# Turning the combine weights in 32x32 blocks on VectorE, and sending the output by thirds of the tokens

## The chip, the cores and the metric

One core of one Trainium2 chip runs the whole program. The metric is the device time of one execution in microseconds (us), taken as the median of several runs. TensorE (PE, with its weight loads shown apart as PEld), VectorE (DVE), ScalarE (ACT), GpSimd (POOL) and the queue engine SyncE (SP) each run their own instruction stream in order; DMA moves data between main memory and the on-chip memories (SBUF, and PSUM, into which TensorE accumulates).

## What is computed

Attention over 4 batches x 8 heads x 768 tokens with head size 64, in which a query sees only the keys whose 6 sign bits equal its own; its output, as 3072 tokens x 512, goes through a soft mixture of 8 experts with 4 slots each. The part that the change touches is the end:

```python
logits = x @ phi                       # 3072 x 32 slots
slot_input = softmax(logits, axis=0).T @ x
for e in range(8):
    slot_out[e] = np.maximum(slot_input[e] @ w1[e], 0) @ w2[e]
c = softmax(logits, axis=1)            # "combine weights", 3072 x 32
out = c @ slot_out                     # 3072 x 512
```

w1 and w2 are 33.5 MB together and come in 64 pieces of 512 KB; the output is 6.3 MB and leaves in 12 pieces of 512 KB.

## The kernel before

**Attention, heads 0 to 31.** Each head takes six "slots" of a hand-made plan: the tables STEADY and ONCE give every step (`smax`, `scores`, `av`, `one_add`, `load_weights` and so on) a time in slots, and the steps are written out in the order of these times, so each engine gets its instructions in that order. `smax` (L418 on TensorE, L421 and L424 on VectorE) finds row maxima, `scores` (L465, exponentials on ScalarE at L469) the weights, `av` (L494) the weighted values. After the last slot of a batch the logits of its 768 tokens are at hand: `batch_weigh` and `batch_share` (L750 to L761) turn them into combine weights and keep them in the SBUF tile `call`, tokens on the partitions.

**End of attention.** Heads 30 and 31 are finished one by one: `one_sum`, `one_turn`, `one_rec`, `one_log`, `one_x` on TensorE, `one_fold` (L623, L624), `one_add` (L630, L634) and `one_put` (L643) on VectorE. Then come the softmax over all tokens (`batch_max` L665, `batch_top`, `batch_fold` L736 to L743) and the slot inputs `siT`.

**Experts.** `hidden` (L904, first layer, groups g = 0 and 1 of four experts), `above_zero` and `turned` (transposes on TensorE, L918), then `model` (L986, second layer) for the left half of the columns (x = 0) and the right half (x = 1). `split_out` (L992 on ScalarE, L993 on VectorE) leaves the slots' outputs as a rounded part and what the rounding left, and `send` (L1008) multiplies them with the turned combine weights `cts`: TensorE into PSUM, VectorE and ScalarE copy out (L1010), SP issues one output piece of 512 KB (L1011) for 128 columns q and 1024 tokens n.

**Turning the combine weights.** `send` needs the slots on the partitions, in a high and a low part. ScalarE and VectorE split `call` into two parts (L934, L935); `arrange` copies them for three blocks of 128 tokens into one tile `avs`, eight small copies shared by VectorE and GpSimd (L943); `turn_weights` turns these blocks by three matmuls with the identity (L949, tile `qa`) and ScalarE copies the result out of PSUM (L950). There are eight such groups (24 blocks); `more_weights(1)` puts one at a time between pieces of `hidden` and `model`, and all eight stand ahead of the first `send`.

**Weights.** `load_weights` asks SP for the next piece (L192 for w1, L194 for w2) as buffers come free: pool wa holds 23, then wb 5, wy 6, wp 3, wl 5 and wc 1 as the tiles of attention are given up, three pieces go into the tile `xq` after its last use, ten into wa after the first `hidden`, eight more after the second. The outputs come behind all of these in SP's stream; six buffers of wy serve them, one of them holding `split_out`'s halves.

Of the kernel before, what the change touches and what calls it, by code (L numbers as in the profile page):

```python
# [9 lines left out]
F32 = mybir.dt.float32  # L10
F32R = mybir.dt.float32r
# [23 lines left out]
N_WA, N_WB, N_WY, N_WP, N_WL, N_WC = 23, 5, 6, 3, 5, 1  # L35
# [43 lines left out]
    ('acc', 31, 1): 189.7, ('acc', 31, 2): 189.705, ('av', 31, 2, 0): 191.864, ('av', 31, 2, 1): 192.733,  # L79
    ('batch_exp', 3): 195.721, ('batch_max', 3): 195.72, ('batch_scale', 3): 195.724, ('batch_top',): 195.7215,  # L80
    ('batch_top_exp',): 195.7222, ('batch_turn', 3): 195.723, ('bits', 2): -3.273955249,
    ('bits_rest',): -37.319143276, ('copy_ident',): -68.066444498, ('first_bits',): -103.791174563,
    ('first_last',): -38.392596163, ('first_mz',): -40.0, ('first_rows', 1): -74.359163702,
    ('first_rows', 2): -26.360163702, ('first_x', 0): -24.334455598, ('first_x', 1): -27.067989537,
    ('first_y', 2): -36.763070462, ('keep_warm', 'a'): -76.154870356, ('keep_warm', 'c'): 195.7225,
    ('load', 10): 37.688669, ('load', 12): 49.688669, ('load', 14): 61.688669, ('load', 2): -12.762070462,
    ('load', 4): 3.305061249, ('load', 6): 13.688669, ('load', 8): 25.688669, ('load_phi',): 10.931086823,
    ('load_v', 0): -61.78673, ('load_weights', 0): 26.669343, ('load_weights', 1): 27.9087,
# [12 lines left out]
    ('scores', 18, 0, 1): 109.396684, ('scores', 20, 0, 1): 121.396684, ('scores', 3, 2, 0): 19.21665,
    ('scores', 5, 2, 0): 31.21665, ('scores', 6, 0, 1): 37.396684, ('scores', 7, 2, 0): 43.21665,
    ('scores', 8, 0, 1): 49.396684, ('scores', 9, 2, 0): 55.21665, ('shift_rows', 0): -3.614750908,
    ('smax', 0, 0, 0): -48.201477503, ('smax', 1, 0, 0): -0.414889731, ('smax', 1, 0, 1): -0.455916355,
    ('smax', 1, 1, 0): -0.415889731, ('smax', 1, 1, 1): -2.391596163, ('smax', 1, 2, 0): 1.521154004,
    ('smax', 1, 2, 1): 0.801484107, ('smax', 1, 3, 0): 0.906213766, ('smax', 1, 3, 1): 0.217376722,
    ('smax', 1, 4, 0): -0.202477503, ('smax', 1, 4, 1): 0.380833062, ('smax', 1, 5, 0): 0.541771494,
    ('smax', 1, 5, 1): -1.142037598, ('split_hi', 2): -7.827923536, ('split_lo', 0, 0): -56.921030823,
    ('split_lo', 0, 1): -46.209390463, ('split_lo', 2, 0): -3.471460996, ('split_lo', 2, 1): -1.544050507,
    ('spread_bits', 1): -11.457228506, ('spread_bits', 2): 2.576813849, ('spread_l', 0): -24.414889731,  # L110
    ('spread_l', 1): -11.211767025, ('spread_l', 2): 9.582727007, ('spread_x', 0): -2.418272993,
    ('spread_x', 1): 3.415989498, ('spread_x', 2): 9.118993846, ('spread_y', 1): -58.753320164,
# [960 lines left out]
```

## Time and profile before

| | us |
|---|---|
| median of 3 runs | 481.88 (481.84 to 482.64) |
| the profiled execution | 480.13 |
| its span (first to last instruction) | 478.4 |
| PE busy | 461.8 (97%) |
| DVE busy | 364.4 (76%) |
| POOL busy | 330.5 (69%) |
| ACT busy | 250.3 (52%) |

The profiled execution is 1.75 us under the median of the runs; about 1.7 us of it lie outside the span. The granted TensorE clock is 1.00 of full speed in every stage from 60 to 470 us. A timeline row gives start, duration, engine, line and operation, the number of merged instructions and in brackets the idle time before it with what ended it. A merged row spans from the first start to the last end.

### The profile page before, as it was taken

To read this page: it belongs to the slowest core of one execution; us is meant where nothing else is said; L and a number is where in the kernel's file an instruction comes from. 1 tells how busy PE (TensorE), PEld (TensorE's weight loads), DVE (VectorE), ACT (ScalarE), POOL (GpSimd) and SP (SyncE) were. 2 spreads that over 40 slices of the span, in tenths; PEclk is the share of its full clock that TensorE was granted. 3 is DMA by queue.
4 is the path that set the end of the run, shared out by engine and by line. 5 is a ranking of instruction groups with operands and counts; after the bars stand their busy time and mean duration, and the time that the engine had idled before them with its cause. 6 is when DMAs were issued, how large, how long until landed. Compare 5 with 4: busy or idle time off the path is not lost.

```text
span 478.4 us, 10738 instructions
## 1 busy us (share of the span) xinstructions
PE 461.8 (97%) x4012; PEld 290.6 (61%) x4012; DVE 364.4 (76%) x690; ACT 250.3 (52%) x465; POOL 330.5 (69%) x236
## 2 busy tenths in 40 slices
PE   7799999999999999999999999999999999989992
PEld 4466666666666666666666565656656666453581
DVE  5658897979798888888888888888989766463242
ACT  4365555564666464555655564646655455431242
POOL 7868776969595969696868696968859696602200
PEclk9799999999999999999999999999999999999998
DMA  5668587868575757777767676767758388979967
GB/s 149 186 164 198 145 180 218 181 170 185 172 174 160 161 136 160 224 173 209 189 168 196 173 216 167 213 166 224 195 169 223 112 214 317 393 295 388 408 267 299
DMA packets 39697, 99.71 MB, mean 208 GB/s; under 512 B 7422, under 2 KB 13708, under 8 KB 39644
## 3 DMA queue, kind: packets, MB, share of 16 engines
q1 hardware_dynamic: 39260, 98.16, 71.6%
q0 software_dynamic: 224, 0.47, 0.5%
q8 instruction: 32, 0.52, 0.5%
q10 hardware_dynamic: 160, 0.39, 0.3%
q14 instruction: 21, 0.17, 0.1%
HBM read 52.76 MB, written 6.29 MB: 123 GB/s over the span
## 4 chain that ended last, share of the span: by engine, by line
PE 90%; DMA 2%; POOL 2%; DVE 2%; issue 1%; ACT 1%; SPq 1%; DVEq 0%; ACTq 0%; POOLq 0%
PE st L465 29%; PE av L494 27%; PE smx L418 15%; PE qh L904 3%; PE mi L556 3%; PE mi L506 2%; PE mi L521 2%; PE qs L986 2%; PE mi L357 2%; DMA out<-w 1%; PE mi L541 1%; PE mi L711 1%; PE qa L949 1%; POOL stage L321 1%; PE mi L449 1%
## 5 line engine op out<-in xcount | busy, mean ns | idle before, releaser
L482 POOL TENSOR_TENSOR acc<-acc,pt 128x768 f32<-128x768 f32 x125 | 229.2, 1834 | 9.1
L469 ACT ACTIVATE pt<-st 128x512 f32<-128x512 f32 x288 | 164.1, 596 | 49.0 <-PE st L465 41.0
L465 PE MATMUL st<-XY 128*128 128x512 f32 (+1 forms) x768 | 180.1, 346 | 0.0
L424 DVE TENSOR_REDUCE mx<-smx 128x1 f32<-128x512 f32 x192 | 130.6, 688 | 28.8 <-PE smx L418 25.3
L465 PEld LDWEIGHTS st<-XY 128*128 128x128 f32 x768 | 129.5, 190 | 16.3 <-issue 0.6
L494 PE MATMUL av<-pt,v 128*32 128x384 f32 x1536 | 136.2, 488 | 0.0
L418 PE MATMUL smx<-XY 96*128 96x256 f32 (+1 forms) x384 | 117.8, 360 | 1.6 <-DMA XY<-bt 0.7
L476 POOL TENSOR_TENSOR acc<-pt 128x768 f32<-128x768 f32 x32 | 58.7, 1835 | 65.8 <-ACT pt L469 65.8
L494 PEld LDWEIGHTS av<-pt,v 128*32 128x32 f32 x1536 | 46.4, 110 | 70.7 <-issue 70.5
L418 PEld LDWEIGHTS smx<-XY 96*128 96x128 f32 x384 | 68.7, 191 | 29.6 <-DVE mx L424 8.8
L421 DVE TENSOR_REDUCE mx<-smx 128x2 f32<-128x512 f32 x96 | 64.8, 675 | 4.3 <-PE smx L418 3.8
L498 ACT COPY avs<-av 128x384 f32<-128x384 f32 x32 | 15.3, 478 | 89.9 <-PE av L494 89.9
L318 DVE TENSOR_REDUCE stage<-stage 128x768 fp32r<-128x1536 f32 x28 | 50.1, 1790 | 0.0
L513 DVE RECIPROCAL sm<-sm 128x128 f32<-128x128 f32 x45 | 38.1, 896 | 0.0
L558 DVE TENSOR_TENSOR xq<-mi,r 128x256 f32<-128x256 f32 x45 | 17.6, 418 | 26.2 <-PE mi L556 26.2
L311 ACT ACTIVATE stage<-stage 128x768 fp32r<-128x768 f32 x30 | 24.9, 840 | 9.0 <-DMA stage<-qk 6.7
L556 PEld LDWEIGHTS mi<-ident,avs 128*128 128x128 f32 x90 | 10.2, 141 | 10.6 <-issue 10.0
L509 ACT ACTIVATE sm<-mi,eps 128x384 f32<-128x384 f32 x15 | 8.7, 582 | 13.8 <-PE mi L506 13.8
L943 POOL CAST avs<-lacc 128x48 fp32r<-128x48 f32 x8 | 2.1, 266 | 19.6 <-ACT lacc L934 12.5
L556 PE MATMUL mi<-ident,avs 128*128 128x128 f32 x90 | 15.7, 282 | 0.0
L986 PE MATMUL qs<-w 128*32 128x128 f32 (+1 forms) x360 | 15.5, 305 | 0.0
L904 PE MATMUL qh<-w,siT 128*32 128x512 f32 x128 | 14.6, 595 | 0.0
(179 smaller groups left out, 334.6 us busy)
## 6 DMA issues: line engine op xcount, KB each, us to landing
w<-w SPq DMA_DIRECT2D x61, 512.0 KB
XY<-stage SPq DMA_DIRECT2D x62, 384.0 KB
stage<-qk SPq DMA_DIRECT2D x32, 384.0 KB
XY<-stage SPq DMA_DIRECT2D x62, 192.0 KB
v<-vt SPq DMA_DIRECT2D x32, 192.0 KB
out<-w SPq DMA_DIRECT2D x12, 512.0 KB
xq<-w SPq DMA_DIRECT2D x3, 512.0 KB
XY<-bt SPq DMA_DIRECT2D x62, 19.5 KB
```

Of the source, the lines that this page charges most:

```text
L318: nc.vector.tensor_reduce(out=w[:, 2 * x + 1], in_=stage[:, x:n + 1:n - x].rearrange("p t s -> p s t"), axis=AX.X, op=ALU.add, negate=True)
L418: nc.tensor.matmul(pt[:, o:o + b - a], Ys[h % N_Y][0:96, 0, t * P:(t + 1) * P], Ys[h % N_Y][0:96, 1, a:b], start=True, stop=True)
L421: nc.vector.tensor_reduce(out=mx[:, n - 1:n + 1], in_=pt.rearrange("p (a x) -> p a x", a=2), axis=AX.X, op=ALU.max)
L424: nc.vector.reduce_max(out=mx[:, n:n + 1], in_=pt, axis=AX.X)
L465: nc.tensor.matmul(pt[:, o:o + b - a], x[:, 1, i * P:(i + 1) * P], x[:, 0, a:b], start=first, stop=not first)
L469: nc.scalar.activation(pts[i // 2][:, 512 * u:512 * u + 512], pt, AF.Exp, scale=D ** -0.5)
L476: nc.gpsimd.tensor_tensor(out=s["acc"], in0=pr[:, 0:S], in1=pr[:, S:2 * S], op=ALU.add)
L482: eng.tensor_tensor(out=s["acc"], in0=s["acc"], in1=pr[:, a * S:(a + 1) * S], op=ALU.add)
L494: nc.tensor.matmul(s["av"][D * c + d:D * c + d + 32, 0:HC], s["v"][:, i, d:d + 32], pr[:, o + c * HC:o + (c + 1) * HC], start=(i == 0), st ...
L513: nc.vector.reciprocal(out=rs[:, k * P:(k + 1) * P], in_=rs[:, k * P:(k + 1) * P])
L556: nc.tensor.transpose(pt[:, o:o + P], st[h + a]["avs"][:, k * P:(k + 1) * P], ident)
L904: nc.tensor.matmul(ph[fh][32 * j:32 * j + 32], siT[:, k, 4 * g + j, :], wt[0, g, k, j][:, fh * 512:(fh + 1) * 512], start=(k == 0), stop=( ...
```

## The change

The combine weights no longer pass through TensorE. `batch_share` now leaves them in `call` already split (one more copy on ScalarE, one more subtraction on GpSimd or, for the last batch, VectorE, both 128x192), laid out so that the 16 numbers of a token for two expert groups lie side by side. `combine(n, j, q)` turns for a third of the plan (n = 0 and 1: nine blocks of 128 tokens each, n = 2: six) one 32-partition strip with a VectorE transpose of 32x32 blocks (L794), `combine_round(n)` copies the turned tile to the matmul's format on ScalarE (L802). Rounds 0 and 1 stand in the plan of attention, at slots 178 to 194; round 2, with the last batch, stands in the expert stage after the transposes of the hidden layer. `phi`'s columns, the folding constant and `siT` are permuted to match.

`send` takes a list of thirds: the first two column quarters go out third by third with pieces of `model` between them, and a part of the third quarter goes out ahead of the last `model`. The output buffers are in wb. Of the weights, wb now takes 7, wy 3, wc 2, and one piece goes into the transposes' tile `cr`; the tile XY2 has a pool of its own (yq), freed early; wa serves 16 instead of 18 later tiles.

```diff
-N_WA, N_WB, N_WY, N_WP, N_WL, N_WC = 23, 5, 6, 3, 5, 1
+N_WA, N_WB, N_WY, N_WP, N_WL, N_WC = 23, 7, 3, 3, 5, 2
...
+    ('combine', 0, 0, 0): 181.507650263, ('combine', 0, 0, 1): 184.14604213, ('combine', 0, 0, 2): 186.99190093,
...
+    ('combine_round', 1): 193.790766733, ('copy_ident',): -68.066444, ('first_bits',): -103.791175,
...
-    call = cp.tile([P, B, 3, 2, NS], F32, name="call")
+    call = cp.tile([P, B - 1, 3, 2, 4, 2, 2 * SPE], F32, name="call")
...
     def batch_share(b):
-        cb = call[:, b]
+        cb, hb = share_of(b), share_of(b, 0).bitcast(F32R)
...
+        nc.scalar.copy(hb, cb)
+        eng.tensor_tensor(out=cb.bitcast(F32R), in0=cb, in1=hb, op=ALU.subtract)
+
+    def combine(n, j, q):
+        t0, t1 = n * N_H, min((n + 1) * N_H, B * NT)
+        if n not in turned_shares:
+            turned_shares[n] = (ep.tile([P, N_H * P], F32, name="cr", bufs=1) if n < 2 else piece())[:, 0:(t1 - t0) * P]
+        o = t0 % (2 * N_H)
+        src = tiles[32 * q:32 * q + 32, o:o + t1 - t0, j]
+        nc.vector.transpose(out=turned_shares[n][32 * j:32 * j + 32].rearrange("r (t q k) -> r t q k", q=4, k=32)[:, :, q],
+                            in_=src[:, :, None].broadcast_to([32, t1 - t0, 2, 4 * SPE]))
+
+    def combine_round(n):
+        if n % 2 == 0:
+            cts[n // 2] = (piece() if n else ep.tile([P, 2 * N_H * P], F32, name="ct")).bitcast(F32R)
+        t = turned_shares[n]
+        o = n % 2 * N_H * P
+        nc.scalar.copy(cts[n // 2][:, o:o + t.shape[1]], t)
...
             free_pp()
+            free_yq()
+            ep = ctx.enter_context(tc.tile_pool(name="ep", bufs=1))
             wb = ctx.enter_context(tc.tile_pool(name="wb", bufs=N_WB))
...
+            load_piece(turned_shares[1][:, 0:F])
             load_weights(wc, N_WC)
...
-    def arrange(t0):
-    def turn_weights(t0, ca):
-    def more_weights(n):
...
     turned(hs1, hT1)
+    for j in range(4):
+        for q in range(4):
+            combine(2, j, q)
+    combine_round(2)
     model(po0, 0, 0, range(4, FC))
-    more_weights(1)
-    model(po0, 0, 1, range(4))
-    more_weights(1)
-    model(po0, 0, 1, range(4, FC))
+    model(po0, 0, 1)
     so0 = split_out(po0, 0)
-    more_weights(1)
     model(po1, 1, 0, range(4), left)
-    more_weights(1)
-    model(po1, 1, 0, range(4, FC), left)
-    more_weights(1)
-    send(so0[:, left], 0)
-    send(so0[:, right], 1)
-    model(po1, 1, 1, cols=left)
+    for n in range(3):
+        send(so0[:, left], 0, (n,))
+        send(so0[:, right], 1, (n,))
+        if n < 2:
+            model(po1, 1, n, range(4 - 4 * n, FC), left)
     so1 = split_out(po1, 1, left)
     po2 = po_tile(P)
     model(po2, 1, 0, cols=right)
-    send(so1, 2)
+    send(so1, 2, (0, 1))
     model(po2, 1, 1, cols=right)
-    send(split_out(po2, 1, right), 3)
+    so2 = split_out(po2, 1, right)
+    send(so1, 2, (2,))
+    send(so2, 3)
```

How the instructions stand on two engines, before and now. VectorE at the end of attention, before, from the last sums of head 31's weights (`acc1`) to the first step that needs head 31's logits (`dl` from `st`); `lacc` holds the batch's logits, `r1` reciprocals of sums:

```order
L482 TENSOR_TENSOR acc1_86<-acc1_86,pt1_83 128x768
L482 TENSOR_TENSOR acc1_86<-acc1_86,pt2_84 128x768
L588 TENSOR_SCALAR r1_4988<-mi_4984 128x6
L592 RECIPROCAL r1_4988<-r1_4988 128x6
L623 COPY sm_5000<-lacc_4324 64x384
L624 TENSOR_TENSOR lacc_4324<-lacc_4324,sm_5000 64x384
L630 TENSOR_TENSOR dl_4951<-dl_4951,mi_5021 64x384
L634 TENSOR_TENSOR lacc_4324<-lacc_4324,dl_4951 64x384
L643 TENSOR_TENSOR xq_4326<-mi_5037,r1_4988 128x3x2x64
L590 COPY r1_5064<-smx_5060 128x6
L591 SCALAR_TENSOR_TENSOR r1_5064<-r1_5064,smx_5060 128x6
L592 RECIPROCAL r1_5064<-r1_5064 128x6
```

VectorE at the same place now; the tile `cr_4988` is the second round's, in the buffer of the first:

```order
L794 STREAM_TRANSPOSE cr_4988<-call_116 32x9x32 x9
L602 TENSOR_SCALAR r1_5029<-mi_5025 128x6
L606 RECIPROCAL r1_5029<-r1_5029 128x6
L496 TENSOR_TENSOR acc1_89<-acc1_89,pt1_86 128x768
L794 STREAM_TRANSPOSE cr_4988<-call_116 32x9x32
L496 TENSOR_TENSOR acc1_89<-acc1_89,pt2_87 128x768
L794 STREAM_TRANSPOSE cr_4988<-call_116 32x9x32
L657 TENSOR_TENSOR xq_4335<-mi_5016,r1_5029 128x3x2x64
L794 STREAM_TRANSPOSE cr_4988<-call_116 32x9x32 x5
L604 COPY r1_5129<-smx_5125 128x6
L605 SCALAR_TENSOR_TENSOR r1_5129<-r1_5129,smx_5125 128x6
L606 RECIPROCAL r1_5129<-r1_5129 128x6
```

Sixteen transposes stand among these steps, and the four steps on `lacc` and `dl` that stood ahead of head 31's reciprocals now follow them, ahead of the step on head 31's logits:

```order
L637 COPY sm_5133<-lacc_4333 64x384
L638 TENSOR_TENSOR lacc_4333<-lacc_4333,sm_5133 64x384
L644 TENSOR_TENSOR dl_4995<-dl_4995,mi_5118 64x384
L648 TENSOR_TENSOR lacc_4333<-lacc_4333,dl_4995 64x384
L644 TENSOR_TENSOR dl_4995<-st_5147,avs_5145 64x384
```

Before, a reciprocal step and a wait for TensorE stood between the fourth of these rows and the fifth; now nothing does.

TensorE before, from the end of the first `model` to the first `send` (`qs` is `model`'s tile, `qa<-ident,avs` one group of turned weights, L1008 the output):

```order
L986 MATMUL qs<-w 32x256 x2
L949 MATMUL qa<-ident,avs 128x128 x3
L986 MATMUL qs<-w 32x128 x16
L949 MATMUL qa<-ident,avs 128x128 x3
L986 MATMUL qs<-w 32x128 x16
L949 MATMUL qa<-ident,avs 128x128 x3
L1008 MATMUL qh<-w 128x512
L1008 MATMUL qh<-w 128x256 x2
L1008 MATMUL qa<-w 128x512
```

TensorE now, from the same place (`ct` and `w` on the right hold the turned weights):

```order
L996 MATMUL qs<-w 32x256
L996 MATMUL qs<-w 32x128 x16
L1018 MATMUL qh<-ct,w 128x512 x4
L996 MATMUL qs<-w 32x128 x16
L1018 MATMUL qa<-ct,w 128x512
L1018 MATMUL qh<-ct,w 128x512
L1018 MATMUL qa<-ct,w 128x512
L1018 MATMUL qh<-ct,w 128x512
L996 MATMUL qs<-w 32x128 x32
```

The groups of three are gone, and the first four output matmuls stand ahead of the second 16 of `model`.

## Rows read from the trace of the kernel before

**Rows 1.** The page's part on the chain of work that ended last: shares of the span by engine.

```profile
PE 90%; DMA 2%; POOL 2%; DVE 2%; issue 1%; ACT 1%; SPq 1%; DVEq 0%; ACTq 0%; POOLq 0%
```

**Rows 2.** Busy time by stretches (start:end, length, then us and instructions for PE, PEld, DVE, ACT and POOL, the granted clock, the DMA share and GB/s), over the end of attention.

```profile
390.00:400.00 10.00, 10.00 (x80) 6.64 (x73) 5.26 (x12) 5.33 (x10) 6.15 (x4) 1.00 0.88 316
400.00:410.00 10.00, 10.00 (x90) 5.55 (x89) 3.97 (x8) 4.98 (x11) 9.77 (x7) 1.00 0.83 318
410.00:420.00 10.00, 10.00 (x100) 4.23 (x100) 5.65 (x14) 3.31 (x7) 3.99 (x4) 1.00 0.97 388
```

**Rows 3.** The chain of work that ended last, merged, in order of time, from 427 us on (start, us, what).

```profile
427.76 8.79 PE qh L904 x80
...
439.43 0.48 PE qa L949 x3
...
455.99 1.01 PE qs L986 x32
457.00 0.48 PE qa L949 x3
457.48 0.53 PE qh L1008 x3
...
460.40 6.65 DMA out<-w
```

**Rows 4.** SP's timeline: when the last weights and the outputs are issued (a merged row spans from the first issue to the last).

```profile
426.24 1.28 SPq L194 DMA_DIRECT2D xq<-w  x3
429.69 17.30 SPq L194 DMA_DIRECT2D w<-w  x18
458.64 13.62 SPq L1011 DMA_DIRECT2D out<-w  x12
```

**Rows 5.** What the DMA engines moved, GB/s in 40 equal slices: first the stretch from 420 to 430 us (slices of 0.25 us), then from 450 to 480 us (slices of 0.75 us).

```profile
GB/s 377 410 442 328 442 328 426 377 393 442 377 442 377 426 426 393 393 131 98 115 82 49 16 0 0 0 0 0 49 66 147 246 442 328 442 361 410 475 360 475
...
GB/s 404 393 410 415 410 415 300 175 49 0 0 11 147 399 404 399 399 382 410 393 399 404 410 388 404 393 388 410 421 410 393 393 437 186 71 16 0 0 0 0
```

**Rows 6.** VectorE's timeline at the end of attention.

```profile
393.28 0.69 DVE L424 TENSOR_REDUCE mx<-smx 128x1 f32<-128x512 f32 x1 [4.20 <-PE smx L418]
...
400.12 2.52 DVE L513 RECIPROCAL sm<-sm 128x128 f32<-128x128 f32 x3
...
405.37 0.42 DVE L558 TENSOR_TENSOR xq<-mi,r 128x256 f32<-128x256 f32 x1 [2.07 <-PE mi L556]
409.65 0.76 DVE L558 TENSOR_TENSOR xq<-mi,r 128x256 f32<-128x256 f32 x2 [3.85 <-PE mi L556]
412.53 2.02 DVE L482 TENSOR_TENSOR acc<-acc,pt 128x768 f32<-128x768 f32 x2 [2.13 <-POOL acc L482]
...
414.88 0.36 DVE L623 COPY sm<-lacc 64x384 f32<-64x384 f32 x1
...
416.47 0.55 DVE L634 TENSOR_TENSOR lacc<-lacc,dl 64x384 f32<-64x384 f32 x1
...
418.27 0.16 DVE L590 COPY r<-smx 128x6 f32<-128x6 f32 x1 [0.71 <-PE smx L584]
...
420.64 0.55 DVE L630 TENSOR_TENSOR dl<-st,avs 64x384 f32<-64x384 f32 x1 [1.79 <-PE st L609]
```

**Rows 7.** VectorE's groups by shape between 388 and 428 us (busy us, mean ns of one, then the idle time before).

```profile
L513 DVE RECIPROCAL sm<-sm 128x128 f32<-128x128 f32 x3 | 2.5, 894 | 0.0
...
L643 DVE TENSOR_TENSOR xq<-mi,r 128x384 f32<-128x384 f32 x1 | 0.6, 557 | 0.0
...
L623 DVE COPY sm<-lacc 64x384 f32<-64x384 f32 x1 | 0.4, 356 | 0.0
...
L590 DVE COPY r<-smx 128x6 f32<-128x6 f32 x1 | 0.2, 164 | 0.7 <-PE smx L584 0.7
```

**Rows 8.** ScalarE: from the page's groups a copy within SBUF to the matmul's format, and two rows of its timeline at the end of attention.

```profile
L311 ACT ACTIVATE stage<-stage 128x768 fp32r<-128x768 f32 x30 | 24.9, 840 | 9.0 <-DMA stage<-qk 6.7
...
405.89 2.60 ACT L469 ACTIVATE pt<-st 128x512 f32<-128x512 f32 x5 [0.38 <-PE st L465]
...
416.61 0.48 ACT L577 COPY sm<-smx 128x384 f32<-128x384 f32 x1 [4.00 <-PE smx L574]
```

**Rows 9.** TensorE's timeline: eight passes of `av`, the transposes of head 31's sums, and its logits.

```profile
416.90 0.85 PE L494 MATMUL av<-pt,v 128*32 128x384 f32 x8
417.69 0.55 PE L584 MATMUL smx<-ident,sm 128*128 128x128 f32 x3
...
419.69 0.83 PE L609 MATMUL st<-avs,phs 64*32 64x384 f32 x4
```

**Rows 10.** The timeline of the expert stage: VectorE's copy of the second turned hidden layer, then the split of the first slot outputs, the first output matmuls and the first copy of an output.

```profile
447.12 0.69 DVE L919 COPY w<-qa 128x512 f32<-128x512 f32 x1 [1.32 <-issue]
...
454.08 0.37 ACT L992 CAST w<-qs 128x256 fp32r<-128x256 f32 x1 [1.42 <-DMA w<-w]
...
454.49 0.48 DVE L993 SCALAR_TENSOR_TENSOR w<-w,con,qs 128x256 fp32r<-128x256 f32 x1 [1.71 <-ACT w L992]
...
457.31 0.68 PE L1008 MATMUL qh<-w 128*128 128x512 f32 x3
...
457.80 0.69 DVE L1010 COPY w<-qh 128x512 f32<-128x512 f32 x1 [2.83 <-PE qh L1008]
```

**Rows 11.** GpSimd's timeline: one elementwise step of 128x384.

```profile
404.08 1.00 POOL L535 TENSOR_TENSOR lacc<-lacc,sm 128x384 f32<-128x384 f32 x1
```

More of the change, by code (lines that the diff above doesn't have):

```diff
@@ L84 @@
[L84 to L88, printed above, removed]
@@ L115 @@
+    ('spread_y', 31): 174.008401,
 }
@@ L265, in lsh_attention_soft_moe @@
     for i in range(N_Y):
-        held = lp if i == (BH - 1) % N_Y else yp
+        held = (yp, lp, yq)[i]
         XYs.append(held.tile([P, 2, 2, S], F32R, name=f"XY{i}"))
@@ L841, in lsh_attention_soft_moe @@
     at(keep_warm, 10, tag="c")
+    for n in range(2):
+        for j in range(4):
+            for q in range(4):
+                at(combine, n, j, q)
+        at(combine_round, n)
     last = NT * BH
@@ L968, in lsh_attention_soft_moe @@
     hs0, hT0 = above_zero(hid[0])
-    cts = [piece().bitcast(F32R) for _ in range(B)]
     hidden(hid[1], 1, range(1))
     turned(hs0, hT0)
-    for k in range(1, KC):
-        hidden(hid[1], 1, range(k, k + 1))
-        more_weights(1)
+    hidden(hid[1], 1, range(1, KC))
     hs1, hT1 = above_zero(hid[1])
     hTs = hT0, hT1
-    for held, n in ((wa, N_WA - 18), (wb, N_WB), (wy, N_WY)):
+    for held, n in ((wa, N_WA - 16), (wb, N_WB)):
         load_weights(held, n)
-    halves = wy.tile([P, F], F32, name="w").bitcast(F32R).rearrange("p (n m) -> p n m", n=4)
+    halves = wb.tile([P, F], F32, name="w").bitcast(F32R).rearrange("p (n m) -> p n m", n=4)
     def model(po, x, g, fs=range(FC), cols=slice(0, HM)):
@@ L995, in split_out, with send @@
         return so
-    def send(so, q):
-        for n in range(B * S // F):
-            ob = wy.tile([P, F], F32, name="w")
+    def send(so, q, ns=range(B * S // F)):
+        for n in ns:
+            ob = wb.tile([P, F], F32, name="w")
             for u in range(2):
@@ L1004, in send @@
                 while at_t < end:
-                    bb, o = divmod(at_t, S)
-                    m = min(end - at_t, S - o)
+                    bb, o = divmod(at_t, (B - 1) * S)
+                    m = min(end, (bb + 1) * (B - 1) * S) - at_t
                     p0 = at_t % 512
@@ L1057 @@
         "first": np.concatenate([pj, constants()[:, 0:C_ID]], axis=1),
-        "phi": np.ascontiguousarray(inputs["moe_phi"]),
+        "phi": np.ascontiguousarray(np.asarray(inputs["moe_phi"]).reshape(DM, 2, 4, SPE).swapaxes(1, 2)).reshape(DM, NS),
         "w1": np.ascontiguousarray(inputs["moe_w1"]),
```

145 lines of the change are left out of this document (71 added, 74 removed).

## The prediction

> **What bounds the kernel now.** I read the chain of work that ended last first: TensorE is 90% of it [rows 1], so in attention a VectorE or ScalarE instruction costs something only where TensorE or the end of a stage waits for it. VectorE is far from full at the end of attention: 5.26 + 3.97 + 5.65 = 14.9 us busy in the 30 us from 390 to 420 [rows 2]. The last 50 us have another bound. There the chain runs along TensorE to the first output matmul at 457.48 and then through a 6.65 us wait for output transfers [rows 3]: SP issues the first output at 458.64, the twelfth at about 472 [rows 4]. The DMA traffic says the same: weights flow at about 400 GB/s until 455, then there is a hole until about 459.6, then the outputs flow at about 400 until 475, after which the span ends at 478.4 [rows 5]. Filling the slices up to 400, the hole is (100 + 225 + 351 + 400 + 400 + 389 + 253) x 0.75 / 400 = 4.0 us [rows 5]. So the end is: first output issue, about 1 us to full flow, 12 pieces at full rate, a fixed rest. A second hole, 424.25 to 428.2, stands between the last load before the end of attention and the loads into `xq` [rows 5, 4].
>
> **Part 1: TensorE loses the eight groups of turned weights.** Each costs 0.48 us in the chain, and eight lie between 437 and 457.48 [rows 3]: 8 x 0.48 = 3.84 us, all of them on the path to the first output. Their copies on VectorE, GpSimd and ScalarE ran beside TensorE and are worth nothing on the path. Half of a `model` (1.01 us, [rows 3]) now also stands behind the first two sends instead of ahead of them. By TensorE alone the first output matmul moves from 457.48 to 457.48 - 3.84 - 1.01 = 452.63.
>
> It also needs `split_out`. The first `model` ended at about 454.0, where the split's row on ScalarE begins [rows 10], with five of the groups ahead of it, so now at 451.6; the split takes from the start of ScalarE's row to the end of VectorE's, 454.08 to 454.97, 0.9 us [rows 10], so 452.55. Both agree. From the first output matmul to the issue it took 458.64 - 457.31 = 1.3 us [rows 10, 4], so issue at about 453.9 instead of 458.64: **4.7 us earlier**, if round 2 of the transposes is out of the way.
>
> **Part 2: what a transpose costs.** No row shows one. It moves 288 numbers per partition on 32 partitions (192 in round 2). Nearest rows: a two-input step over 384 takes 557 ns, a plain copy over 384 takes 356, and one over 6 or 12 about 164, which is the fixed part [rows 7]. So (557 - 164) / 384 = 1.02 ns per number at the ordinary rate and about 0.5 for a plain copy. At the ordinary rate a transpose of 288 is 0.16 + 0.29 = 0.46 us, one of 192 is 0.36; at the copy's rate 0.31 and 0.26; if each number took two beats, 0.75 and 0.55. The far end is the reciprocal, 894 ns for 128, some 5.7 ns per number [rows 7], which I set aside since nothing here is computed. Independent instructions overlap: three reciprocals of 0.894 take 2.52, a pitch of 0.81, 0.08 less than one [rows 6, 7]. I take the ordinary rate: **0.38 us** per transpose at the end of attention, 0.28 in round 2.
>
> In the Trainium skill, the page "Vector Engine (DVE) Microarchitecture Reference", section "The reshape front-end and per-opcode configuration", has the 32x32 array sustain one element per cycle and lane; no run here shows it yet, and it speaks against the two beats.
>
> **Part 3: rounds 0 and 1 at the end of attention.** Sixteen transposes of round 0 are 6.1 us of VectorE; they lie in its gaps: 4.2 us before the row of 393.28, then 2.1 and 3.9 us before two more rows that wait for TensorE [rows 6]. Some of the others stand between row maxima whose gaps are 0.2 to 0.5 us each; I allow 0.2 us of delay for these and for the three extra GpSimd subtractions of 128x192 (half of a 1.0 us step each, [rows 11]), on an engine that is not the bound.
>
> ScalarE's copy of 128x1152 is, from 840 ns for 128x768 [rows 8], about 1.2 us. The first stands among exponentials that run almost back to back from 405.89 [rows 8], but TensorE has three PSUM buffers for them and the next steps need these exponentials only after 412: nothing. VectorE's round 1 must wait for that copy, since it writes the same buffer: round 0 ends at about 407.9 (five transposes behind the 405.37 row), the copy at about 409.2. The second copy falls into ScalarE's idle stretch after 416.61 [rows 8].
>
> Round 1 is on the path. From 409.65 (two `xq` steps, now a little earlier): nine transposes to about 413.0, reciprocals 0.4, the two sums of head 31 (2.02 together, [rows 6]) with one transpose between them to about 415.9, then a transpose, one `xq` step of 0.56, five transposes: VectorE is free at about 418.8. TensorE comes with head 31's turned sums at 418.2 before [rows 9]; one more group of eight `av` passes (0.8 us, [rows 9]) stands ahead of it now, so 419.0. They meet: VectorE's transposes just fit. But the four steps on `lacc` and `dl`, 414.88 to 417.02, 2.14 us [rows 6], which filled a wait before, now follow the three reciprocal steps: 419.0 + 0.6 + 2.14 = 421.75, against 420.64 for the first step on head 31's logits [rows 6]. TensorE's logits would be there at 421.2. So the end of attention moves by **+1.1 us**, and all that follows with it, the `xq` loads and `hidden` included. That part does not depend on the transposes as long as one has a pitch under 0.42 us.
>
> **Part 4: round 2 in the expert stage.** It starts after VectorE's copy that ended at 447.81 [rows 10], now three groups earlier, 446.4: 16 x 0.28 = 4.5, to 450.9; ScalarE's copy of 128x768 0.84 [rows 8], to 451.7, just when `split_out` wants ScalarE (451.6). Cost 0.1; the `model` pieces cover it, and beyond a pitch of about 0.28 it costs 16 times the excess.
>
> **Part 5: supply of the outputs.** Weights end at 455 less 1.3 us (one piece more is loaded before the end of attention, and the hole at 424 shrinks by that), so they do not stand in the outputs' way. The pairs of outputs then come at TensorE's pace, with 1.0 to 2.0 us of `model` between them, and twelve pieces at 1.26 us each (15.1 us of flow after 459.6) need one issue every 1.26. From the pieces' places in TensorE's order I get issues at 453.9, 454.6, 456.0, 456.6, 458.8, 459.4, 461.4, 462.0, 464.0, 464.8, 465.5 and 466.2 (before part 3's delay); needed are 453.9 + 1.26 k, so 458.9, 461.5 and 464.0 for the fifth, seventh and ninth, which come just in time. I allow **0.4 us** for small holes. Buffers: six as before.
>
> **Sum** against the profiled execution, 480.13 (span 478.4): -4.7 + 0.1 + 0.2 + 1.1 + 0.4 = -2.9 us, so 477.2 there. The median is 1.75 us above the profiled execution, which I keep: 481.88 - 2.9 = **479.0**.
>
> **Rivals.**
> *Slow transposes (slower than before).* At two beats per number (pitch 0.68 and 0.48): round 1 ends VectorE's run at 423.3, then 0.6 + 2.14, 426.0, so attention ends 5.4 us late; round 2 ends at 454.1, the copy at 454.9, the split at 455.9, the issue at 457.2, so 1.4 us is left of the 4.7. Together 5.4 + 0.4 + 0.2 - 1.4 = +4.6, about 486.5. Each 0.1 us of pitch beyond the free 0.42 and 0.28 costs 1.6 us in each of the two places; the gain is gone at about 0.49 us per transpose of 288. For it: broadcast reads in runs of 16 numbers and writes in runs of 32, shapes that no row has. Against: rows with strided operands here keep the ordinary rate. Chance 0.14.
> *No overlap.* With the full 0.46 and 0.36 as pitch, attention ends 1.9 us late and round 2 costs 1.3: -4.7 + 1.3 + 1.9 + 0.2 + 0.4 = -0.9, about 481.0. Chance 0.12. The Trainium skill ("VectorE: DVE Perf Modes", "The three transpose paths" and "Rules for kernel authors") gives 390 ns for a 128x128 transpose on TensorE, 311 ns on VectorE, there only in 32x32 blocks, and advises TensorE for a full 128x128 where PSUM will do; as an estimate, its 311 ns for 128 numbers plus 160 more at 1.02 ns is 0.47 us, which is this rival. Its advice compares the engines alone; in this trace TensorE is the engine that is waited for [rows 3].
> *The outputs run dry.* If each of the four later groups of outputs leaves a hole of about 0.5 us, 2.0 instead of 0.4: -1.3, about 480.6. Chance 0.14.
> *Attention is not delayed.* If the `lacc` steps find cover and supply is perfect: -4.7 + 0.7 = -4.0, about 477.9. Chance 0.15.
> *The output does not start early*, because something else holds `send` (a buffer of wb, a late weight): SP's order still has all loads first [rows 4], but the last is issued by 447; what is left is part 3 alone, about +1, 483. Chance 0.04.
>
> **How the numbers follow.** The forecast has 0.41. A measurement of this kernel tells about 0.2%, 0.96 us, from no change. Faster: the forecast, no delay, and two fifths of the dry and overlap cases, 0.41 + 0.15 + 0.10 = 0.66. Within 0.2%: the rest of those two, 0.16, and the mild end of the slow transposes, 0.02. Slower: 0.16. The range reaches from no delay (477.8) past no overlap to the mild end of the slow cases, 482.0; some 0.1 lies above it and 0.05 below.
>
> **What would show it.** L794 at 0.45 us or less, pitch below 0.4; no L949; VectorE's first step on head 31's logits about 1 us later than 420.64; the first output issued at about 455.2, 3.4 us earlier than 458.64; no hole of 4 us between weights and outputs, at most one of 1.5; the output transfers ending near 472. Transposes of 0.5 us or more, or holes among the outputs, would prove the sum wrong; so would a TensorE waiting for row maxima between 390 and 402.

## Result and profile after

The changed kernel takes 484.32 us (median of 12 runs, 482.57 to 488.76) beside 481.86 (12 runs, 480.64 to 483.22) for the kernel before on the same chip: a ratio of 1.0063, 95% interval [1.0041, 1.0085]. It is **slower**, by 3.0 us [2.0, 4.1] by this ratio (the two medians alone are 2.5 us apart), where 479.0 had been forecast and 482.0 was the end of the range.

I cut both profiled executions at the same four events: ScalarE's copy of head 30's `av` sums, the first matmul of `hidden`, the first issue of an output, the end of the span. "Heads" is the time from the start to that copy. The spans are read to 0.1 us, so the last column of stages is good to 0.05.

| us | heads | copy to `hidden` | `hidden` to first output | first output to end | span |
|---|---|---|---|---|---|
| before | 405.03 | 22.73 | 30.88 | 19.76 | 478.4 |
| after | 409.69 | 25.20 | 27.31 | 19.80 | 482.0 |
| difference | +4.66 | +2.47 | -3.57 | +0.04 | +3.6 |

The last three columns give -1.06 us together. The loss is in the first, a stage for which the prediction had 0.2 us. Of its 4.66 us, 1.34 are there at head 0 already, ahead of the first step that the change adds, and the profiled run of before lies 1.7 us under its median: that part is chance. It goes with TensorE's clock. In the first 28 us the granted clock is at 0.50 of full speed (1.2 GHz instead of 2.4) for 6.8 us in before and 10.2 in after. In the twelve runs below it is there for 3.4 to 17.1 us, and their head 0 ends from 0.6 us earlier to 2.2 us later than in before; e3 and e9, which change nothing that early, are among the latest. The other 3.3 us come in steps: 0.3 at head 12, 1.07 at head 20, 1.3 at head 23, 0.6 from head 28 to 30.

**Where the heads lose time.** ScalarE, SP and GpSimd of after around the end of the second batch of heads, from their timelines (start, us, engine, line, operation, idle time before it and what ended it):

```profile
255.68 0.35 ACT L781 CAST call<-call 128x192 fp32r<-128x192 f32 x1 [2.27 <-POOL call L779]
255.94 0.25 ACT L466 CAST mr<-mi 12x128 fp32r<-12x128 f32 x1
...
255.14 0.51 POOL L779 TENSOR_TENSOR call<-call,cs 128x192 f32<-128x192 f32 x1 [1.70 <-DVE cs L778]
256.11 0.60 POOL L782 TENSOR_TENSOR call<-call 128x192 fp32r<-128x192 f32 x1 [0.46 <-ACT call L781]
...
256.22 0.74 SPq L339 DMA_DIRECT2D XY<-mr  x1
257.06 0.72 SPq L339 DMA_DIRECT2D XY<-stage  x1
257.83 3.46 SPq L339 DMA_DIRECT2D XY<-bt  x4
261.33 4.58 SPq L339 DMA_DIRECT2D XY<-stage  x5
266.01 1.86 SPq L339 DMA_DIRECT2D XY<-mr  x1
```

The same place in before:

```profile
251.98 0.25 ACT L452 CAST mr<-mi 12x128 fp32r<-12x128 f32 x1 [0.20 <-PE mi L449]
...
252.26 0.75 SPq L325 DMA_DIRECT2D XY<-mr  x1
...
257.46 4.66 SPq L325 DMA_DIRECT2D XY<-stage  x5
264.31 0.83 SPq L325 DMA_DIRECT2D XY<-mr  x1
```

L781 is the new copy that splits a batch's combine weights. It waits 2.27 us for GpSimd, and the cast of the row maxima (`mr`), ready long before, stands behind it on ScalarE. Measured from head 19's copy, which is 1.63 us later in after, `mr` is 2.3 us late, SP's order starts with its DMA, and ten transfers follow it by as much. In before SP was done with them 2.2 us ahead of the next `XY<-mr`; in after that one is issued right behind them and lands after 5.92 us; in before the same transfer, issued at 264.31, landed after 2.00. TensorE then waits 0.85 us for it. From after's chain of waits, then from TensorE's timeline:

```profile
266.01 5.92 DMA XY<-mr
```

```profile
272.06 1.16 PE L479 MATMUL st<-XY 128*128 128x512 f32 x4 [0.85 <-DMA XY<-mr]
...
310.86 1.19 PE L479 MATMUL st<-XY 128*128 128x512 f32 x4 [1.04 <-DMA XY<-mr]
```

Before has no such wait. The second one, at 310.86, is behind the step at head 23, and that it comes from the copy is not shown: no batch's weights are split near it, the `mr` transfer that it waits for took 6.77 us, and the same transfer took 4.55 in before and 5.96 in e9 below, which has no copy on ScalarE. By ScalarE's groups in after, the copy has its wait after each batch (6.8 us in the first three; after the last it is shorter and for VectorE):

```profile
L781 ACT CAST call<-call 128x192 fp32r<-128x192 f32 x4 | 1.4, 352 | 8.0 <-POOL call L779 6.8 <-DVE call L779 1.2
```

**The transposes.** VectorE's groups by shape in after (busy us, mean ns of one, idle before), its timeline at the end of attention, and busy time by stretches as in [rows 2], then one such row of before and one of after, each from the copy of head 30's sums to `hidden`:

```profile
L794 DVE STREAM_TRANSPOSE cr<-call 32x288 f32<-32x288 f32 x32 | 15.0, 470 | 4.1 <-DMA XY<-mr 3.1 <-ACT ct L802 0.4
...
L794 DVE STREAM_TRANSPOSE w<-call 32x192 f32<-32x192 f32 x16 | 5.9, 369 | 0.2
```

```profile
414.76 4.34 DVE L794 STREAM_TRANSPOSE cr<-call 32x288 f32<-32x288 f32 x9 [0.43 <-ACT ct L802]
...
425.89 0.35 DVE L637 COPY sm<-lacc 64x384 f32<-64x384 f32 x1
...
428.01 0.55 DVE L644 TENSOR_TENSOR dl<-st,avs 64x384 f32<-64x384 f32 x1
```

```profile
390.00:400.00 10.00, 9.99 (x81) 6.06 (x80) 6.69 (x15) 4.80 (x11) 8.90 (x5) 1.00 0.85 246
400.00:410.00 10.00, 10.00 (x94) 5.82 (x93) 9.52 (x21) 4.85 (x10) 6.22 (x4) 1.00 0.84 302
410.00:420.00 10.00, 9.88 (x77) 5.62 (x79) 9.24 (x22) 6.60 (x13) 7.54 (x5) 1.00 0.59 222
420.00:430.00 10.00, 7.51 (x81) 4.61 (x74) 9.40 (x22) 2.58 (x4) 1.57 (x2) 1.00 0.99 375
```

```profile
405.03:427.76 22.73, 21.46 (x198) 12.41 (x197) 12.08 (x37) 9.29 (x20) 8.88 (x7) 1.00 0.86 337
...
409.69:434.89 25.20, 21.21 (x198) 12.78 (x197) 22.70 (x61) 11.26 (x22) 9.42 (x7) 1.00 0.84 320
```

Nine transposes take 4.34 us, a pitch of 0.48: the 470 ns of one and no overlap. VectorE, half idle in [rows 2], is busy for 9.2 to 9.5 of each 10 us from 400 to 430 (third figure behind the length). Over the whole stretch from the copy to `hidden` VectorE's busy time goes from 12.08 to 22.70 us, and TensorE, which has the same work, idles 3.99 us instead of 1.27 (length less first figure). The chain on `lacc`, which was done at 417.02 in before [rows 6], starts at 425.89, and the first step on head 31's logits at 428.01 has no idle time left ahead of it; in before it waited 1.79 us for TensorE [rows 6].

**The tail.** ScalarE's, VectorE's, TensorE's and SP's timelines of after at the first output, then what the DMA engines moved from 450 to 480 us, to be set against the second row of [rows 5]:

```profile
459.15 0.83 ACT L802 CAST w<-w 128x768 fp32r<-128x768 f32 x1 [5.74 <-DVE w L794]
459.88 0.37 ACT L1002 CAST w<-qs 128x256 fp32r<-128x256 f32 x1
...
453.00 6.11 DVE L794 STREAM_TRANSPOSE w<-call 32x192 f32<-32x192 f32 x16
460.28 0.48 DVE L1003 SCALAR_TENSOR_TENSOR w<-w,con,qs 128x256 fp32r<-128x256 f32 x1 [1.17 <-ACT w L1002]
...
460.82 1.19 PE L1018 MATMUL qh<-ct,w 128*128 128x512 f32 x4 [1.89 <-DVE w L1003]
...
462.20 14.19 SPq L1021 DMA_DIRECT2D out<-w  x12
```

```profile
GB/s 393 421 415 388 426 410 399 388 431 393 393 415 421 410 355 131 22 257 404 399 410 399 399 415 371 399 404 290 322 393 421 295 284 410 410 399 410 415 399 120
```

The hole between weights and outputs shrank from 4.0 us to (45 + 269 + 378 + 143) x 0.75 / 400 = 1.6. What is left is round 2: its sixteen transposes end at 459.11, ScalarE's copy of the turned piece at 459.98, the split of the first outputs queues behind it, and TensorE waits 1.89 us for the split.

### The profile page after: what moved, and what is told of

The parts are those of the page before. It is cut to its first block, busy times and chain, and to the rows that moved or that the text cites. A ratio compares the mean times of both kernels' runs of the same rounds, so it can differ in the third digit from the quotient of the medians.

```text
span 482.0 us, 10641 instructions
## 1 busy us (share of the span) xinstructions
PE 461.4 (96%) x3984; PEld 288.5 (60%) x3984; DVE 379.9 (79%) x705; ACT 248.6 (52%) x462; POOL 326.3 (68%) x207
## 4 chain that ended last, share of the span: by engine, by line
PE 84%; DMA 8%; DVE 5%; ACT 1%; issue 1%; DVEq 0%; SPq 0%
PE st L479 27%; PE av L508 24%; PE smx L432 15%; DMA w<-w 3%; PE qh L954 3%; DMA XY<-mr 3%; PE mi L520 2%; PE mi L570 2%; PE mi L371 2%; PE mi L535 2%; DVE cr L794 1%; PE qs L996 1%; DMA cr<-w 1%; DVE mx L438 1%; PE mi L555 1%; PE mi L725 1%
## 5 line engine op out<-in xcount | busy, mean ns | idle before, releaser
L794 DVE STREAM_TRANSPOSE cr<-call 32x288 f32<-32x288 f32 x32 | 15.0, 470 | 4.1 <-DMA XY<-mr 3.1
L570 PEld LDWEIGHTS mi<-ident,avs 128*128 128x128 f32 x90 | 10.3, 141 | 10.1 <-issue 8.8
L549 POOL TENSOR_TENSOR lacc<-lacc,sm 128x384 f32<-128x384 f32 x11 | 11.1, 1006 | 4.7 <-DVE sm L547 4.7
```

What stands on the lines that cost most here:

```text
L570: nc.tensor.transpose(pt[:, o:o + P], st[h + a]["avs"][:, k * P:(k + 1) * P], ident)
```

## Experiments

Column 2 is the ratio to the kernel before with its interval; the rest comes from each one's profiled execution, cut as above. "Growth" is how much later head 30 is than head 19 against before; "waits" is TensorE's waits for `XY<-mr` after the second batch of heads.

| kernel | ratio | growth | waits | copy to `hidden` | `hidden` to output | output to end |
|---|---|---|---|---|---|---|
| after | 1.0063 [1.0041, 1.0085] | 3.03 | 1.89 | 25.20 | 27.31 | 19.80 |
| e1_late_round1 | 0.9994 [0.9963, 1.0024] | 1.20 | 0.73 | 23.50 | 27.43 | 20.65 |
| e2_chain_first | 0.9996 [0.9979, 1.0013] | 4.65 | 2.39 | 22.91 | 27.45 | 19.55 |
| e3_thirds_only | 1.0004 [0.9983, 1.0026] | 1.31 | 1.09 | 22.72 | 29.06 | 21.23 |
| e4_front_only | 1.0039 [1.0012, 1.0066] | 1.09 | 0.70 | 22.72 | 30.88 | 19.68 |
| e5_pool_yq_only | 0.9991 [0.9970, 1.0012] | 0.35 | 0 | 22.72 | 30.88 | 19.78 |
| e6_split_only | 1.0045 [1.0023, 1.0068] | 3.96 | 2.78 | 22.73 | 30.89 | 19.72 |
| e7_old_places | 0.9980 [0.9960, 1.0001] | 2.31 | 1.75 | 22.87 | 27.43 | 20.41 |
| e8_split_once | 0.9957 [0.9941, 0.9973] | 0.20 | 0 | 22.81 | 27.43 | 20.66 |
| e9_split_on_gpsimd | 1.0003 [0.9988, 1.0018] | 0.53 | 0.23 | 22.73 | 30.89 | 19.68 |
| e10_copy_without_subtract | 1.0035 [1.0015, 1.0056] | 1.13 | 0.59 | 22.73 | 30.88 | 19.81 |
| e11_late_third_copy | 0.9938 [0.9911, 0.9965] | 0.32 | 0 | 22.80 | 26.30 | 21.50 |
| e8_again | 0.9948 [0.9930, 0.9966] | -0.04 | 0 | 22.80 | 27.43 | 19.63 |

Growth and waits are of one execution each, so the ratios decide on them; e3, without any split, had a wait of 1.09 us too, and e6's profiled execution is the slowest of its twelve (487.21 us, median 483.89).

The last column holds chance as well: e8_split_once and e8_again are one kernel and differ by 1.03 us there. Ahead of the first output TensorE waits 2.01 us for the split in e1, e2, e7 and both e8. In e1 and e8_split_once the granted clock then falls to 0.50 of full speed (1.2 GHz); in e2, e7 and e8_again it stays at 1.00 (2.4 GHz). The next 32 matmuls of `model`, first in e8_split_once, then in e8_again, and the stretch from 456.5 to 459.5 in both:

```profile
456.70 1.93 PE L1007 MATMUL qs<-w 128*32 128x128 f32 x32
...
456.82 1.08 PE L1007 MATMUL qs<-w 128*32 128x128 f32 x32
```

```profile
456.50:459.50 3.00, 3.00 (x35) 2.19 (x35) 0.89 (x3) 0.89 (x2) 0.00 (x0) 0.50 0.96 385
...
456.50:459.50 3.00, 3.00 (x58) 2.04 (x60) 2.15 (x4) 1.94 (x4) 0.00 (x0) 1.00 0.96 385
```

**e1_late_round1**: after, with round 1's transposes moved out of the end of attention into the expert stage, half before `hidden` and half behind the first `turned`.

```diff
-    for n in range(2):
-        for j in range(4):
-            for q in range(4):
-                at(combine, n, j, q)
-        at(combine_round, n)
+    for j in range(4):
+        for q in range(4):
+            at(combine, 0, j, q)
+    at(combine_round, 0)
...
-            load_piece(turned_shares[1][:, 0:F])
...
     batch_share(B - 1)
+    for j in range(2):
+        for q in range(4):
+            combine(1, j, q)
...
     turned(hs0, hT0)
+    for j in range(2, 4):
+        for q in range(4):
+            combine(1, j, q)
+    combine_round(1)
```

> The changed kernel with round 1 of the transposes moved out of attention into the expert stage, where VectorE idles under the hidden layer (the one weight piece that went into the transposes' tile is loaded last instead). Theory A, VectorE was full at the end of attention: the changed kernel has 16 transposes at a pitch of 0.48 us there, 7.7 us, between 414.8 and 425.3, with no idle time around them; without them the stretch from the last head's values (av of head 31) to the first hidden matmul falls from 11.4 us (8.7 in the kernel before) to about 9.8, what the reordered lacc steps cost, and the time to about 482.5. Theory B, the loss lies in the heads before (start, row moves, GpSimd), and TensorE bounds the end of attention anyway: that stretch stays at 11.4 and the time at about 484.

Copy to `hidden` falls by 1.70 us: that is what sixteen transposes cost at the end of attention, together with ScalarE's copy behind them and the early load of one weight piece, which went with them.

**e2_chain_first**: e1, with the chain on `lacc` ahead of VectorE's wait for head 31 again (three entries of the table ONCE).

```diff
-('one_add', 30): 217.271144
+('one_add', 30): 192.2
-('one_fold', 3): 209.580487
+('one_fold', 3): 191.29
-('one_rec', 30): 201.899393422
+('one_rec', 30): 191.62
```

> As e1_late_round1, and the steps on lacc and dl of heads 30 and 31 stand again ahead of head 31's reciprocals, as in the kernel before. Theory A with the term of the prediction (2.14 us of serial VectorE steps moved behind the wait): another 1.1 us off the stretch from av of head 31 to the first hidden matmul, to about 8.7 us, and 1.1 us off the time of e1_late_round1, about 481.4. Rival: the four steps were hidden in e1_late_round1 too, no change against it.

Another 0.59 us, for the chain's place once the transposes are gone; 22.91 is within 0.2 of before. Yet e1 and e2 as wholes are no faster than before, though their three late stages are 1.8 and 3.5 us shorter. Something ahead of them takes it back.

**e3_thirds_only**: before, with the outputs sent by thirds; the groups of turned weights stay on TensorE.

```diff
+    for n in range(3):
+        send(so0[:, left], 0, (n,))
+        send(so0[:, right], 1, (n,))
+        if n < 2:
+            more_weights(1)
+            model(po1, 1, n, range(4 - 4 * n, FC), left)
```

> The kernel before with nothing but the outputs sent by thirds: matmul transposes stay, two of the eight groups and half a model now stand behind the first sends. Theory, TensorE's order sets the first output issue and the hole in the DMA traffic is real time: 2 x 0.48 + 1.01 = 2.0 us earlier, about 480.0 against 481.9. Rival, outputs wait behind the weights' traffic or run dry later: no change, 481.9. The heads run as in the kernel before in either case.

The first output leaves 1.82 us earlier, the outputs take 1.47 longer: sending by thirds alone is worth nothing that these runs can tell. The twelfth output is issued 43.16 us behind the first matmul of `hidden`, and 43.44 in before: what TensorE has to do ahead of the last output is the same.

**e4_front_only, e5_pool_yq_only, e6_split_only**: before, with both edits of the attention stage, with the third XY tile's own pool alone, with the split steps alone. In e4 and e6, and in e9 and e10 below, the split shares go to a tile that nothing reads.

```diff
-        held = lp if i == (BH - 1) % N_Y else yp
+        held = (yp, lp, yq)[i]
...
+        hb, lb = (spare[:, n].bitcast(F32R) for n in range(2))
+        nc.scalar.copy(hb, cb)
+        eng.tensor_tensor(out=lb, in0=cb, in1=hb, op=ALU.subtract)
```

> The kernel before with what the change adds before slot 178 and nothing else: the split of the combine weights after each batch (a ScalarE copy and a GpSimd, for the last batch VectorE, subtraction of 128x192; results unused) and a pool of its own for XY2, freed with the others. In the changed kernel's profile head ends lag the kernel before by 1.33 us from head 0, +0.25 at head 12, +1.07 at head 20, +1.3 at head 23, +0.34 at head 28. Theory A, the extra GpSimd steps push its backlog: lags appear at heads 12, 20 and 28, 0.3 us each, time +0.8, about 482.7. Theory B, the tiles' new places slow the row moves: late rows at single heads as in the changed kernel, time +2 or more, 484. Theory C, start and row moves are chance: nothing of it, 481.9.

> The kernel before with the tile XY2 in a pool of its own, freed together with the others; nothing else. e4_front_only (this and the split steps) was 0.39% slower than the kernel before. Theory A, the tiles' places cost it: 0.3 to 0.4% slower, about 483.2. Theory B, the split steps cost it: same as before, 481.5.

> The kernel before with only the split of the combine weights after each batch (ScalarE copy, GpSimd subtraction, results unused). Theory B, these steps cost the time, by GpSimd's backlog and by the row moves that come later for it: 0.3 to 0.4% slower, about 483.2. Theory A, the tiles' places do: same as before, 481.5.

The pool alone: no difference. The split alone: +0.45%, 2.2 us [1.1, 3.3], with all late stages as before. Of the two edits it is the split steps that cost the time.

**e9_split_on_gpsimd and e10_copy_without_subtract**: is it ScalarE's wait, or the extra step on GpSimd? e9 is e6 with the copy on GpSimd; e10 is e6 without the subtraction.

```diff
-        nc.scalar.copy(hb, cb)
+        eng.tensor_copy(hb, cb)
```

```diff
-        eng.tensor_tensor(out=lb, in0=cb, in1=hb, op=ALU.subtract)
```

> The kernel before with the two split steps for each batch as in e6_split_only (the split shares are written to a tile that nothing reads), but the copy of the upper part is done by GpSimd (for the last batch by VectorE), so nothing of the split stands in ScalarE's order. Theory A (what costs time is ScalarE: its copy waits 2.3 us for GpSimd's multiply and stands ahead of the row cast that TensorE's next scores need): within 0.1% of the kernel before, the jumps of 0.7 to 1.6 us at heads 20 and 21 gone, no wait of ScalarE on the shares. Theory B (what costs time is GpSimd: the extra step holds its next accumulations back): as slow as e6_split_only, +0.45%, or slower, about 484.0 to 485.0, since GpSimd now has two extra steps for each batch.

> The kernel before with ScalarE's copy of the shares alone (into a tile that nothing reads), no subtraction on GpSimd. Theory A (ScalarE's blocked order): as slow as e6_split_only, +0.3 to 0.45%, with jumps at heads 20 and 21, ScalarE waiting 2 us on the shares. Theory B (GpSimd's extra step): within 0.1% of the kernel before.

ScalarE's timeline, first e9, then e10:

```profile
254.20 0.26 ACT L453 CAST mr<-mi 12x128 fp32r<-12x128 f32 x1 [0.20 <-PE mi L450]
```

```profile
255.56 0.35 ACT L764 CAST spare<-call 128x192 fp32r<-128x192 f32 x1 [2.27 <-POOL call L762]
255.82 0.25 ACT L453 CAST mr<-mi 12x128 fp32r<-12x128 f32 x1
```

e9, with two extra steps on GpSimd for each batch, takes as long as before (+0.03%, interval -0.12% to +0.18%); e10, with none there but the copy on ScalarE, is 0.35% slower, 1.7 us [0.7, 2.7]; the medians are 482.11 and 483.25. Theory B falls. Taking away head 19's delay (2.24 and 1.52 us), e9's `mr` is cast at 251.96, as in before, and e10's at 254.30.

The other profiles say the same. The `mr` transfer that follows the late ten landed 4.34 to 5.92 us after its issue in the seven kernels that have ScalarE's copy after each batch (after, e1, e2, e4, e6, e7, e10), and 2.00 to 2.75 us in the seven executions without it (before, e3, e5, both e8, e9, e11). From head 19 to head 21 the first seven fall 0.8 to 2.3 us further behind before, the others at most 0.02.

**e7_old_places**: e2, with the XY tiles and the last weights' buffers in the pools of before.

```diff
-N_WA, N_WB, N_WY, N_WP, N_WL, N_WC = 23, 7, 3, 3, 5, 2
+N_WA, N_WB, N_WY, N_WP, N_WL, N_WC = 23, 4, 6, 3, 5, 2
...
-        held = (yp, lp, yq)[i]
+        held = lp if i == (BH - 1) % N_Y else yp
```

> As e2_chain_first, with XY0 and XY2 in one pool as in the kernel before (wb 4, wy 6 buffers; outputs in wy). From the stage table e2_chain_first is 3.5 us shorter than the kernel before from the end of head 30 to the end, yet its time is the same, so its heads cost about 3 us more on average. If the places do that: about 479.0. If the split steps or something else do: about 481.5, as e2_chain_first.

0.9980 against 0.9996: the intervals overlap, so the new places cost nothing that these runs can tell.

**e8_split_once** (and **e8_again**): e7, with the split of the first three batches made at once, at the end of attention, by one ScalarE copy and one VectorE subtraction over 128x576.

```diff
+    def part_shares():
+        cf = call.rearrange("p b k c j h i -> p (b k c j) h i")
+        hb, cb = cf[:, :, 0].bitcast(F32R), cf[:, :, 1]
+        nc.scalar.copy(hb, cb)
+        nc.vector.tensor_tensor(out=cb.bitcast(F32R), in0=cb, in1=hb, op=ALU.subtract)
...
+    at(part_shares)
     for j in range(4):
         for q in range(4):
             at(combine, 0, j, q)
```

> As e7_old_places, and the three batches' combine weights are split in one ScalarE copy and one VectorE subtraction of 128x576 just before round 0, no GpSimd step after a batch. If the split steps cost the heads' time: about 478.5, some 0.6% under the kernel before. If neither the steps nor the places do: 481.5, as e2_chain_first.

> e8_split_once once more, beside the other three: again 0.3 to 0.5% below the kernel before.

With the three copies gone from between the heads, TensorE's waits are gone, the growth is 0.20 and -0.04 us, and the kernel is faster than before and after: 480.08 and 478.88 us, 0.43% and 0.52% below before.

**e11_late_third_copy**: e8, with ScalarE's copy of the third turned piece behind the first split.

```diff
-    combine_round(2)
     model(po0, 0, 0, range(4, FC))
     model(po0, 0, 1)
     so0 = split_out(po0, 0)
+    combine_round(2)
```

> e8_split_once with ScalarE's copy of the third piece of turned weights (128x768, 0.83 us) behind the split of the first outputs instead of ahead of it. The first two sends read only the first two pieces' tokens. Theory: the last wait ahead of the first output matmul is ScalarE's queue, where the split stands behind this copy: TensorE was done with its model passes at 453.5 in e8_split_once, the split began at 454.53. So the first output is issued 0.9 us earlier, and the kernel takes about 0.8 us less than e8_split_once beside it. Rival: the two casts and copies of the first outputs on ScalarE now queue behind the 0.83 us copy instead, so that the second half of the first output is late by as much: no difference.

The first output is issued 1.13 us earlier, counted from `hidden`, and the kernel does not gain that could be told: 0.9938 [0.9911, 0.9965] beside e8's 0.9948 [0.9930, 0.9966]. The rival's queue on ScalarE is not the reason: ScalarE idles 0.47 us ahead of its copy of the first output. TensorE's timeline of e11 shows where the gain goes, then a piece of its chain:

```profile
460.09 0.41 PE L1007 MATMUL qs<-w 128*32 128x128 f32 x2 [0.72 <-DMA w<-w]
461.35 1.06 PE L1007 MATMUL qs<-w 128*32 128x128 f32 x26 [0.85 <-DMA w<-w]
```

```profile
449.84 11.46 DMA w<-w
```

TensorE, which is at the last weights sooner than in e8, waits 1.57 us for them; in both e8 it has no wait at that place. The twelfth output is issued 41.79 us behind `hidden`, 40.72 in e8_again. The last piece, issued at 449.84, landed after 11.46 us; in e8_again, issued at 449.8 too, after 10.20. That the outputs, issued from 456.20 on, slow these loads is not shown: pieces that landed at 454 already took half a microsecond longer than in e8_again, and in e2 and e7 the first output is issued 3 to 4 us ahead of the last landing and the piece takes 10.1 to 10.2 us.

## Why the prediction was wrong

The step that failed is in **Part 3**: "I allow 0.2 us of delay for these and for the three extra GpSimd subtractions". It costed the split steps as work on an engine that is not the bound, named only the subtractions, and gave ScalarE's three copies of 128x192 no line at all. Their work is 0.35 us each; their price is the wait of 2.27 us with which they block ScalarE's order, behind which stood the cast that starts SP's next eleven transfers. That this wait, and not GpSimd's step, costs the time is shown by e9 and e10 together: 1.7 us [0.7, 2.7] for the copy alone (e10), 2.2 [1.1, 3.3] for both steps (e6), instead of 0.2. The same copy as mere work, made once for three batches where its input is there (e8), costs nothing that shows. The instructions in question read from a tile that GpSimd had yet to write, and `mr` was the next of ScalarE's list in the order; both could be seen ahead.

**Part 1** had the right size: 4.7 us, and e11, in which round 2's copy no longer stands ahead of the split, has 30.88 - 26.30 = 4.58. Even there TensorE waits 0.88 us for the split, which Part 1 had arriving just in time, so part of the agreement is luck. **Part 2** had the right duration, 0.46 against 0.470 us, 0.36 against 0.369, and the wrong pitch: 0.48 and 0.38 instead of 0.38 and 0.28. The overlap of 0.08 was read from three reciprocals and does not hold for transposes. Each transpose reads and writes another 32-partition strip than the one before it, while the reciprocals are all on the same 128 partitions; whether that is the reason was not tried. The difference of the two sizes is (470 - 369) / 96 = 1.05 ns per number, the ordinary rate of [rows 7]. That agrees with the one element per cycle and lane of the Trainium skill ("Vector Engine (DVE) Microarchitecture Reference", "The reshape front-end and per-opcode configuration"): there are no two beats. The estimate of 0.47 us from the Trainium skill's 311 ns ("VectorE: DVE Perf Modes", "The three transpose paths"), which that page gives for bf16 and not for the fp32 of this kernel, is close to the 0.470 measured.

So for the late stages the rival **No overlap** was what happened: it had +1.9 for attention, -3.4 for the tail and 0.4 for supply, -1.1 together, against +2.47, -3.57 and +0.04, -1.06 measured. That the totals agree so closely is luck, since the terms do not and the last one can move by 1 us with the clock. In detail, the chain on `lacc` cost 0.59 (e2) instead of **1.1**, the transposes 1.70 (e1) instead of nothing. **Part 4**: round 2 cost 1.1 us (e11 against e8) instead of 0.1. **Part 5**: the outputs ran as fast as before in after, 19.80 against 19.76, with the twelfth issued 40.43 us behind `hidden` instead of 43.44; in e3 and e11 they did not.

Sum in the profiled executions: 1.34 (start, chance) + 3.32 (heads) + 2.47 - 3.57 + 0.04 = +3.6, where -2.9 had been forecast. Of these 6.5 us the heads make 3.1, the end of attention 1.4, round 2 ahead of the first output 1.0 and the start 1.3; the outputs give 0.4 back. So the split steps are the largest part of the miss and the pitch the next: with the heads' 3.1 alone the forecast would have been 482.1, with the pitch's 2.4 alone 481.4, both about the end of its range or inside. What stays open: the late stages' -1.06 and e6's +2.2 make +1.1 where the ratio says 3.0 [2.0, 4.1], while the profile's own 3.3 for the heads makes +2.3, inside. Three things could fill the gap and were not told apart: the 1.3 us at head 23, which no run ties to the split; a lower clock behind the wait ahead of the first output in some executions of after, as in e1 and e8_split_once, worth about 1 us; and a higher price of the split with the new places of the buffers (e2 against e7 leans that way).

## What to carry to other kernels

An instruction added to an in-order engine costs its wait as well as its work, and the wait falls on what is queued behind it: list that, above all a small step that releases DMAs, and ask how long the new instruction's input will be missing. Place such a step where its input is already there (e8), or on the engine that produces the input (e9). And an output that starts earlier gains nothing by itself: in e3 the work ahead of the last output stayed the same, in e11 the next weights were not there yet.

## What the runs showed of the hardware

Transposes of 32x288 follow each other on VectorE at 0.48 us with 0.47 each, those of 32x192 at 0.38 with 0.37, while reciprocals overlap by 0.08 [rows 6, 7]. The granted clock fell to 0.50 of full speed behind a wait of 2.01 us of TensorE in two of five executions (e1, e8_split_once), and the outputs ended about 1 us later for it.

In e8_again one VectorE subtraction of 128x576 took 1.49 us, where 128x192 takes 0.36; at that row's 1.03 ns per number beyond the fixed 0.16 it would be 0.75. It is not slower by the number: it began while a step of GpSimd was running, and ended 0.62 us behind that step's end at 392.78. In e8_split_once and e11 the same two ends are 0.62 and 0.61 us apart. GpSimd's next step took 2.22 us, where the one before took 1.83. So the two engines look as if they had waited for each other; no run tests it. VectorE's groups, then VectorE's and GpSimd's timelines of e8_again:

```profile
L789 DVE TENSOR_TENSOR call<-call 128x576 fp32r<-128x576 f32 x1 | 1.5, 1486 | 1.0 <-ACT call L788 1.0
...
L783 DVE TENSOR_TENSOR call<-call 128x192 fp32r<-128x192 f32 x1 | 0.4, 357 | 0.4 <-ACT call L782 0.4
```

```profile
391.91 1.49 DVE L789 TENSOR_TENSOR call<-call 128x576 fp32r<-128x576 f32 x1 [1.02 <-ACT call L788]
...
390.95 1.83 POOL L496 TENSOR_TENSOR acc<-acc,pt 128x768 f32<-128x768 f32 x1
...
392.86 2.22 POOL L496 TENSOR_TENSOR acc<-acc,pt 128x768 f32<-128x768 f32 x1
```
